# Casting loads of v on GpSimd's queue, wider early ReLUs and paired score phases in a linear-attention and MLP kernel

## The chip, the cores and the metric

The kernel runs on one core of one Trainium2 chip. The metric is the device time in microseconds (us) of one execution, smaller is better; where several executions were timed, the median is given. Two of the core's data paths matter here beside its compute engines: SP (SyncE) issues DMAs on one queue (q1 in the profile), GpSimd (POOL) issues them on another (q0).

## The reference

Two stages are computed, one after the other. Shapes: 4 batches, 8 heads, 768 steps, head size 48; 3072 tokens of 384 features, hidden size 2048. All inputs and the output are float32.

```python
def _attn_ref(q, k, v, alpha):
    state = np.zeros((B, H, D, D), dtype=np.float32)
    for t in range(S):
        state = alpha[:, :, t, :, None] * state + np.einsum('bhd,bhe->bhde', k[:, :, t], v[:, :, t])
        y[:, :, t] = np.einsum('bhd,bhde->bhe', q[:, :, t], state)
    return y

def _moe_ref(x, w_in, w_out):          # x: y with the heads side by side
    r = np.maximum(x @ w_in, 0.0)
    return (r * r) @ w_out
```

## The kernel before

**Tiles.** The 3072 tokens are 24 chunks of 128 steps, six to a batch. For each chunk the recurrence is done in closed form: the logarithm of alpha is summed along the steps on TensorE, its exponential A scales q and the inverse Ainv scales k, masked products of the two give the weights of v within the chunk, and a state carried from chunk to chunk gives the rest. The result is transposed into `xT_big` and is the input of the MLP ("MoE" in the code).

**One chunk** (`add_chunk`) is a chain over the engines. The names are those of the planned operations: `e_ln` (ScalarE, L445); `p0`, the sums (TensorE); `e_A`, `e_Ai`, `e_ae0`, `e_ae1`, exponentials (ScalarE, L461 to L471); `e_qA`, `e_kI`, the scaled q and k (VectorE, L474 and L477; for the first four chunks `e_kI` may go to GpSimd); `p1`, their transposes (TensorE), copied by `e_cp`; `p2`, the scores, eight matmuls of 64 rows (TensorE, L521); `e_sm`, the causal mask on the scores, two multiplies of 512 columns (VectorE, L536); `ps`, the state's update, then `e_stm` and `e_sb`; `p3`, mask times v plus q times state; `e_xn`; `p4`, the transposes; `e_xT`. v is read by `ps` and `p3` in bfloat16: `e_vb` (L441) casts the loaded float32 tile on GpSimd.

**The first four chunks** share a start of their own (`four_slots`): alpha and q of the first 512 steps come as two larger loads each (`slot_at`, `slot_qt`, L322), four steps to a partition, so that the sums of all four chunks are made at once. The order of these chunks' operations is written out by hand as priorities in the table `RANK`.

**The MLP.** Tokens are taken in groups of one or two chunks (`GN`). In `add_moe1` one *fill* is three matmuls of up to 256 columns into a PSUM bank for one of 16 blocks of the hidden size, followed by a ReLU on ScalarE (`e_relu`, L640) and a square on VectorE (`e_sq`, L646) into `gT`. In `add_moe2` sixteen matmuls of 384 columns per token tile make the output, which is copied out of PSUM (`e_ev`, L678) and stored by SP (L683). All matmuls are recorded at the helper's line L225, transposes at L228.

**Loads and queues.** `add_loads` issues at, qt, kt and vt (alpha, q, k, v) of a chunk, 192 KB each, from SP (L336); chunks 4 and 5 are issued by GpSimd through `pool_dma`, which keeps GpSimd's loads in a chain. The weights are loaded by GpSimd as well, cast to bfloat16 on the way, in four quarters each (`load_w`, L289). `hold_w` (L304) holds the first weight load until chunk 2's keys have landed; `hold_x` (L310) holds chunk 6's alpha, the first of SP's later loads, until chunk 5's keys have landed. Each of the four load tiles has `LB = 5` buffers.

**What sets the order.** Every operation is an `Op` with an engine, an assumed duration, what it depends on and a priority. `Plan.run` walks through time with these durations and takes on each engine whatever can start first, then by priority; the resulting order is emitted and pinned, so each engine runs its instructions in that fixed order and waits where the chip differs from the plan. Seven PSUM banks are handed out by the same plan: from chunk 6 on, the linear attention uses banks 0 and 1 (`GLA_BANKS`) for `p0`, `p1`, `p3` and `p4`, and banks 5 and 6 (`sl_sc`) for the scores; the MLP uses the three between. A chunk may start only `LEAD = 4` chunks ahead of the MLP's progress (`gate`).

Of the kernel before, what the change touches and what calls it, by code (L numbers as in the profile page):

```python
# [8 lines left out]
FP32 = mybir.dt.float32  # L9
# [101 lines left out]
def kernel(  # L111
# [32 lines left out]
    LB = 5  # L144
    loads = ctx.enter_context(tc.tile_pool(name="loads", bufs=LB))
# [81 lines left out]
    def tr(*a):  # L227
# [4 lines left out]
        "ps0": -59.649, "kI0": -59.644, "xn2": -57.597, "stm2": -57.593, "vb1": -57.593, "vb3": -57.587,  # L232
        "cpq2": -57.587, "Ai1": -57.583, "pq1": -57.579, "stm0": -55.864, "kI2": -52.641, "qA2": -52.000,
        "sm0": -51.992, "cp2": -51.977, "xT3": -51.974, "sm3": -51.974, "A0": -49.635, "qA0": -49.458,
        "xn1": -49.452, "pk": -48.562, "p42": -48.558, "p13": -48.116, "p43": -47.738, "xT2": -47.629,
        "qA1": -45.851, "cp1": -45.808, "cpq3": -44.752, "ae0": -42.850, "ae1": -42.842, "cpq0": -42.695,
        "sb1": -40.290, "vb0": -39.263, "p21": -37.946, "pq2": -37.716, "kI3": -37.711, "p33": -37.384,
        "xT1": -37.379, "ps1": -37.280, "tq2": -36.745, "pq3": -36.029, "cp0": -33.098, "sb2": -33.092,
        "ln1": -32.725, "kI1": -32.161, "A3": -32.154, "tq1": -32.145, "stm1": -31.966, "Ai3": -31.587,
        "p40": -31.579, "p30": -31.562, "p32": -30.816, "A1": -29.621, "tq0": -23.589, "qA3": -23.487,  # L240
        "sb0": -23.373, "Ai2": -23.199, "pq0": -22.649, "ln0": -22.507, "sm2": -22.167, "sb3": -20.897,
        "p41": -20.599, "sm1": -18.297, "A2": -15.473, "p12": -13.495, "vb2": -13.438, "Ai0": -12.640,
        "p23": -12.616, "ps3": -12.587, "xn0": -11.830, "cp3": -10.020, "p20": -10.018, "pae": -10.015,
        "xT0": -9.291, "tq3": -8.768, "p22": -7.414, "stm3": -7.367, "p11": -7.059, "ps2": -5.829, "p31":
        -5.636, "p10": -4.409, "cpq1": -2.002, "xn3": -0.260,
# [32 lines left out]
    hold = consts.tile([P, 1], FP32)  # L278
    w_gate = []

    def pool_dma(dur, issue, emit, *deps):

        i = add("POOL", issue, emit, *deps, *w_gate, prio=-50.0, lat=0.0)
        w_gate[:] = [i]
        return add("DMA", dur, lambda: None, i, lat=2.0)
# [16 lines left out]
    def hold_w(d, nm):  # L302
        def e_hold():
            pin(nc.gpsimd.tensor_copy(hold, d[nm][:, 0, 0:1]))  # L304
        w_gate[:] = [add("POOL", 0.1, e_hold, d["ld_" + nm], prio=-6.0)]

# [5 lines left out]

    C = [dict() for _ in range(NT)]
# [3 lines left out]
    def load_tile(nm):  # L317
        return loads.tile([P, H, D], FP32, name=nm)

    def load_slots(nm, lo, hi):  # L320
        def ld():
            pin(nc.sync.dma_start(out=slot[nm][:, lo:hi].rearrange("p h j d -> p h (j d)"),  # L322
                                  in_=slot_srcs[nm][:, lo:hi]))
        return add("DMA", 2.4 * (hi - lo) / H, ld, lat=2.0, at=0.9)

    def add_loads(s, names=("at", "qt", "kt", "vt"), pool=False):
        d = C[s]
        b, c = divmod(s, NCH)
        for nm, src in srcs:
            if nm not in names:  # L330
                continue

            def ld(nm=nm, src=src):
                if nm not in d:
                    d[nm] = load_tile(nm)
                pin((nc.gpsimd if pool else nc.sync).dma_start(out=d[nm], in_=src[b, c]))  # L336
            m = made[nm]
            prev = C[m[-LB]]["use_" + nm] if len(m) >= LB else None
            m.append(s)
            if pool:  # L340
                d["ld_" + nm] = pool_dma(LD, X_ISSUE, ld, prev)
# [3 lines left out]
    def four_slots(ld_at, ld_qt):  # L345
# [19 lines left out]
        pks = add("PE", 1.0, e_pk, *pk, key="pk", prio=-31.0)  # L365
# [26 lines left out]
        for j in range(NJ):  # L392
# [23 lines left out]
            pq = e["pq_"] = add("PE", 0.65, e_pq, *lns, takes=sl_all, key=f"pq{j}", **h)  # L416
# [8 lines left out]
    def add_chunk(s):  # L425
# [13 lines left out]
        def e_vb():  # L439
            d["vb"] = work.tile([P, H, D], BF16, name="vb", bufs=4)  # L440
            pin(nc.gpsimd.tensor_copy(d["vb"], d["vt"]))  # L441
        vb = d["use_vt"] = add("POOL", 0.52, e_vb, d["ld_vt"], old, key=key("vb"), prio=-60.0 if s < 6 else -5.0)
# [46 lines left out]
        if first:  # L489
            lo = NP  # L490
            ae1 = d["aes"]
            mk = d["use_kt"] = add({"DVE": 0.47, "POOL": 0.92}, 0, e_kI, d["ai"], d["ld_kt"], key=key("kI"), **g)
# [44 lines left out]
        if s < 6:  # L537
            p2s = [add("PE", 0.3, lambda hh=hh: e_p2h(hh), cp, *q_ready, takes=sl_all, key=key("p2"), **g) for hh in range(2)]
            sm_after = p2s
        else:  # L540
            p2s = [plan.add(Op("PE", 0.0, lambda hh=hh: e_sc_bank(hh), [cp], takes=[sl_sc[hh]], lat=0.0, **g)) for hh in range(2)]
            sm_after = [add("PE", 0.42, e_p2, *p2s, **g)] * 2
# [5 lines left out]
        if not last:  # L548
            def e_ps():
# [3 lines left out]
                for p in range(NP):  # L553
                    mm(st[:, p, :], lhsT=kI[:, 2 * p:2 * p + 2, :], rhs=d["vb"][:, 2 * p:2 * p + 2, :],
# [16 lines left out]
        def e_p3():  # L571
# [5 lines left out]
            for hh in range(2):  # L577
                for p in range(NP):
                    h = 2 * p + hh
                    mm(py[:, h * D:(h + 1) * D], lhsT=d["sm"][:, hh, p, :], rhs=d["vb"][:, h, :],  # L580
# [22 lines left out]
        d["end"] = d["x"]  # L603

# [20 lines left out]
    def add_moe1(g, f, before):  # L625
        t0, n = GT[g] * P, GN[g] * P
        box = {}

        def e_mm():
            prog_t = box["ph"] = psum(op, [P, 512], FP32)  # L630
# [163 lines left out]
```

## Time and profile before

| | |
|---|---|
| median of 9 runs | 194.36 us (191.01 to 195.92) |
| the profiled execution | 193.66 us, of which the profile's span is 192.0 us |
| TensorE matmul (PE) busy | 180.8 us, 94% of the span |
| VectorE (DVE), ScalarE (ACT), GpSimd (POOL) busy | 140.2, 132.9, 33.9 us |
| first MoE matmul | at 20.88 us of the span |
| last matmul's output copy | starts at 188.46 us |
| loads of at, qt, kt, vt by SP | 18, 18, 22, 22 |
| casts of v on GpSimd | 24, 14.3 us in all |
| ReLUs | 208, 70.3 us in all |

The profile shows one execution. "Busy" sums the instructions of an engine without double counting; the end of a matmul is modelled, so starts are the firmer numbers. Times inside the span start at its zero; 1.66 us of the execution lie outside it. The chain is read backwards from the last instruction: at each step it names what released it.

### The profile page before, as it was taken

What the parts mean: (1) busy time and instruction counts of PE and PEld (TensorE: products, weight loads), DVE (VectorE), ACT (ScalarE), POOL (GpSimd) and SP (SyncE); (2) the same over time, 40 slices, a digit from 0 to 9 for tenths busy, and PEclk for the clock granted to TensorE, in tenths of its full rate; (3) what the DMA queues carried; (4) which work ended last, traced back from release to release, by engine and by line L of the source; (5) the groups of instructions that cost most, each with busy time, mean ns of one, the idle gap of its engine ahead of it and who ended that gap; (6) DMA issues with size and microseconds to landing.
All of it is one profiled execution on the core that took longest, in us unless ns stands there. A gap on an engine that the chain in (4) does not pass through costs nothing.

```text
span 192.0 us, 5309 instructions
## 1 busy us (share of the span) xinstructions
PE 180.8 (94%) x1973; PEld 133.8 (70%) x1973; DVE 140.2 (73%) x380; ACT 132.9 (69%) x393; POOL 33.9 (18%) x64
## 2 busy tenths in 40 slices
PE   7769899999989996999999999999999999999992
PEld 2346688667776874777777787787777777777751
DVE  3199778548999996787888888888798887754400
ACT  3665799356895985787787788688787677556610
POOL 7079835211011211111111011011010000000000
PEclk9999999999999999999999999999999999999999
DMA  6997999959978997999999847845011011011112
GB/s 183 241 199 116 174 205 236 239 116 224 234 169 169 203 229 144 209 203 231 208 202 224 175 104 162 160 104 151 5 41 41 3 41 42 3 41 46 41 41 82
DMA packets 93017, 27.07 MB, mean 141 GB/s; under 512 B 83904, under 2 KB 92608, under 8 KB 92992
## 3 DMA queue, kind: packets, MB, share of 16 engines
q1 hardware_dynamic: 88768, 22.03, 51.6%
q0 software_dynamic: 4224, 4.72, 14.2%
q8 instruction: 15, 0.25, 0.6%
q14 instruction: 10, 0.08, 0.1%
HBM read 25.17 MB, written 4.72 MB: 156 GB/s over the span
## 4 chain that ended last, share of the span: by engine, by line
PE 82%; DMA 8%; SPq 4%; ACT 2%; POOL 1%; issue 1%; ACTq 0%
PE bank L225 75%; PE bank L228 6%; DMA w_in_b<-in_moe_w_in_dram 3%; DMA at<-in_alpha_dram 3%; SPq L336 3%; DMA vt<-in_v_dram 2%; PE st L225 1%; SPq L322 1%; ACT r L640 1%; POOL kI_s L477 1%; POOL vb L441 1%; ACT L_s L445 0%; ACT xn L219 0%; ACT ob L678 0%; ACT A L461 0%
## 5 line engine op out<-in xcount | busy, mean ns | idle before, releaser
L640 ACT ACTIVATE r<-bank 128x256 bf16<-128x256 f32 (+1 forms) x208 | 70.3, 373 | 27.4 <-PE bank L225 26.7
L225 PE MATMUL bank<-xT_big,w_in_b 128*128 128x256 bf16 (+1 forms) x624 | 79.8, 264 | 1.7 <-DMA w_in_b<-in_moe_w_in_dram 0.8
L225 PE MATMUL bank<-w_out_b,gT 128*128 128x384 bf16 x384 | 75.0, 326 | 0.0
L646 DVE TENSOR_TENSOR gT<-r 128x256 bf16<-128x256 bf16 (+1 forms) x208 | 55.5, 289 | 14.8 <-ACT r L640 13.2
L225 PEld LDWEIGHTS <-w_in_b 128*128 128x128 bf16 x624 | 52.8, 97 | 10.1 <-issue 1.0
L225 PEld LDWEIGHTS <-gT 128*128 128x128 bf16 x384 | 36.8, 98 | 16.5
L441 POOL CAST vb<-vt 128x384 bf16<-128x384 f32 x24 | 14.3, 597 | 94.6 <-PE bank L225 59.4
L536 DVE TENSOR_TENSOR sm<-bank,utri_b 128x512 bf16<-128x512 f32 x40 | 27.0, 685 | 3.8 <-PE bank L225 3.8
L217 DVE COPY qkT<-bank 128x1024 bf16<-128x1024 bf16 (+1 forms) x21 | 14.2, 675 | 6.0 <-PE bank L228 6.0
L678 ACT COPY ob<-bank 128x384 f32<-128x384 f32 x21 | 10.0, 478 | 10.5 <-PE bank L225 10.5
L474 DVE TENSOR_TENSOR qA_s<-qt,A 128x384 bf16<-128x384 f32 x20 | 11.4, 572 | 6.4 <-ACT A L461 6.3
L225 PEld LDWEIGHTS <-qkT 64*128 64x128 bf16 (+1 forms) x260 | 10.4, 95 | 7.0 <-DVE gT L646 3.8
L568 ACT CAST sb<-st 128x384 bf16<-128x384 f32 x20 | 9.6, 481 | 5.4 <-DVE st L563 5.3
L445 ACT ACTIVATE L_s<-at 128x384 bf16<-128x384 f32 x20 | 10.3, 522 | 3.4 <-DMA at<-in_alpha_dram 3.1
L477 DVE TENSOR_TENSOR kI_s<-kt,Ainv 128x384 bf16<-128x384 f32 x22 | 12.1, 549 | 0.4 <-ACT Ainv L465 0.3
L219 ACT CAST xn<-bank 128x384 bf16<-128x384 f32 x22 | 10.8, 491 | 1.6 <-PE bank L225 1.5
L563 DVE TENSOR_TENSOR st<-st,ae_s 128x384 f32<-128x384 f32 x20 | 11.1, 556 | 0.7 <-PE st L225 0.7
L461 ACT ACTIVATE A<-bank 128x384 bf16<-128x384 f32 x20 | 9.9, 497 | 1.0 <-PE bank L225 1.0
L465 ACT ACTIVATE Ainv<-bank 128x384 bf16<-128x384 f32 x20 | 10.5, 525 | 0.0
L228 PE MATMUL bank<-ident_bf,qA_s 128*128 128x128 bf16 x96 | 9.3, 219 | 1.2 <-DVE qA_s L407 0.8
L228 PEld LDWEIGHTS <-qA_s 128*128 128x128 bf16 x96 | 6.9, 98 | 4.0 <-DVE qA_s L407 2.0
L225 PE MATMUL bank<-vb,sm 128*128 128x48 bf16 x192 | 9.0, 184 | 0.4 <-DVE sm L536 0.3
(77 smaller groups left out, 158.7 us busy)
## 6 DMA issues: line engine op xcount, KB each, us to landing
out_dram<-ob SPq DMA_DIRECT2D x24, 192.0 KB, 2.9
kt<-in_k_dram SPq DMA_DIRECT2D x22, 192.0 KB, 3.7
vt<-in_v_dram SPq DMA_DIRECT2D x22, 192.0 KB, 3.9
at<-in_alpha_dram SPq DMA_DIRECT2D x18, 192.0 KB, 4.1
qt<-in_q_dram SPq DMA_DIRECT2D x18, 192.0 KB, 3.7
w_in_b<-in_moe_w_in_dram POOLq DMA_DIRECT2D x4, 384.0 KB, 7.6
w_out_b<-in_moe_w_out_dram POOLq DMA_DIRECT2D x4, 384.0 KB, 11.1
slot_at<-in_alpha_dram SPq DMA_DIRECT2D x2, 384.0 KB, 3.8
```

The source lines that it names most:

```text
L217: pin(nc.vector.tensor_copy(out, in_))
L219: pin(nc.scalar.copy(out, in_))
L225: pin(nc.tensor.matmul(*a, **kw))
L228: pin(nc.tensor.transpose(*a))
L441: pin(nc.gpsimd.tensor_copy(d["vb"], d["vt"]))
L465: pin(nc.scalar.activation(d["Ai"], d["pm"][:, 0:HD].rearrange("p (h d) -> p h d", h=H), AF.Exp, scale=-1.0))
L474: pin(nc.vector.tensor_mul(qA[:, :, 0:D], d["qt"], d["A"]))
L477: pin((nc.vector if mk.eng == "DVE" else nc.gpsimd).tensor_mul(kI[:, :, 0:D], d["kt"], d["Ai"]))
L536: pin(nc.vector.tensor_mul(d["sm"][:, hh], d["sc"][hh], (utri_p if first else utri_b).to_broadcast([P, NP, P])))
L563: pin(nc.vector.tensor_mul(st4, st4, bcast(ae, D)))
L640: pin(nc.scalar.activation(box["r"][:, 0:n], box["ph"][:, 0:n], AF.Relu))
L646: pin(nc.vector.tensor_mul(gT[g][:, f, 0:n], box["r"][:, 0:n], box["r"][:, 0:n]))
```

## The change

- **v.** `e_vb` and the float32 tile of v are gone. v is loaded into a bfloat16 tile (`LBV = 6` buffers) and cast by the DMA, for all 24 chunks from GpSimd's queue. From chunk 6 on, a one-column copy on GpSimd stands ahead of each such load and makes it wait for the previous chunk's keys; the buffer is free when `p3` of six chunks before is done.
- **The start.** Chunk 3's keys are issued by GpSimd too, ahead of v3 and of the weights; `hold_w` is gone, the four quarters of `w_in` follow at once. `e_kI` of the first four chunks stays on VectorE. `RANK` is replaced. Ten more dummy matmuls, of 128 columns, follow the nine of 512 at the start.
- **Chunk 6** is held until chunk 5's alpha has landed, not its keys.
- **ReLUs.** In the first five groups (`g < M1_ALT`) `nf` fills go side by side into one bank of 512 columns (two fills for groups of two chunks, four for groups of one), then one ReLU and one square take them all.
- **Scores.** From chunk 10 on (`PAIRS`), the scores of an even chunk and of the next are made in one phase, sixteen matmuls one after the other; the even chunk's use banks 5 and 6, the odd one's banks 0 and 1.
- **The last output tile** is made in two halves of 192 columns, each over all sixteen blocks. The second half is copied out by VectorE and ScalarE, 96 columns each, and stored from two queues.
- Some assumed durations of the plan change slightly.

```diff
+    LBV = 6
...
     RANK = {
...
-    def hold_w(d, nm):
-        def e_hold():
-            pin(nc.gpsimd.tensor_copy(hold, d[nm][:, 0, 0:1]))
-        w_gate[:] = [add("POOL", 0.1, e_hold, d["ld_" + nm], prio=-6.0)]
...
+    PAIRS = 10
     def load_tile(nm):
+        if nm == "vt":
+            return loads.tile([P, H, D], BF16, name=nm, bufs=LBV)
         return loads.tile([P, H, D], FP32, name=nm)
...
             def ld(nm=nm, src=src):
                 if nm not in d:
                     d[nm] = load_tile(nm)
-                pin((nc.gpsimd if pool else nc.sync).dma_start(out=d[nm], in_=src[b, c]))
+                if nm == "vt" and after:
+                    pin(nc.gpsimd.tensor_copy(d[nm][:, 0, 0:1], after["kt"][:, 0, 0:1]))
+                pin((nc.gpsimd if pool or nm == "vt" else nc.sync).dma_start(out=d[nm], in_=src[b, c]))
...
-        def e_vb():
-            d["vb"] = work.tile([P, H, D], BF16, name="vb", bufs=4)
-            pin(nc.gpsimd.tensor_copy(d["vb"], d["vt"]))
-        vb = d["use_vt"] = add("POOL", 0.52, e_vb, d["ld_vt"], old, key=key("vb"), prio=-60.0 if s < 6 else -5.0)
+        vb = d["ld_vt"]
...
-            mk = d["use_kt"] = add({"DVE": 0.47, "POOL": 0.92}, 0, e_kI, d["ai"], d["ld_kt"], key=key("kI"), **g)
+            mk = d["use_kt"] = add("DVE", 0.47, e_kI, d["ai"], d["ld_kt"], key=key("kI"), **g)
...
+            second = s % 2
+            p2s = [add("PE", 0.0, lambda hh=hh: e_sc_bank(hh), cp, takes=[(GLA_BANKS if second else sl_sc)[hh]],
+                       lat=0.0, **g) for hh in range(2)]
+            if second:
+                p2 = C[s - 1]["p2"]
+                for o in C[s - 1]["p2s"]:
+                    o.deps.append(cp)
+                p2.deps += p2s
+                p2.both = e_p2
+            else:
+                def e_both():
+                    e_p2()
+                    p2.both()
+                p2 = add("PE", 0.63, e_both, *p2s, **g)
...
+    def moe1_fill(g):
+        return 512 // (GN[g] * P) if g < M1_ALT else 1
...
         def e_relu():
-            box["r"] = rpool.tile([P, 512], BF16, name="r")
-            pin(nc.scalar.activation(box["r"][:, 0:n], box["ph"][:, 0:n], AF.Relu))
+            box["r"] = rpool.tile([P, nf, n], BF16, name="r")
+            pin(nc.scalar.activation(box["r"], box["ph"], AF.Relu))
...
+    def add_last_tile(g, tt, before):
+        w = d_model // 2
+        for half in range(2):
...
+            parts = [("DVE", 0, w)] if half == 0 else [("DVE", 0, w // 2), ("ACT", w // 2, w // 2)]
...
     for s in range(NJ):
-        add_loads(s, ("kt", "vt"))
-        if s == 3:
-            hold_w(C[2], "kt")
-            load_w_in(0)
+        add_loads(s, ("kt", "vt"), pool=s == NJ - 1)
...
-    for x in "iiioo4oo5":
+    for x in "iiiioo4oo5":
...
-    hold_x(C[6], C[5], "kt")
+    hold_x(C[6], C[5], "at")
     for s in range(6, NT):
-        add_loads(s)
+        add_loads(s, after=C[s - 1])
...
     dummies(9, 0.0, 1.0)
+    dummies(10, 0.0, 1.0, 128)
```

## The prediction

> **What bounds the kernel now.** I read the page first (busy shares, chain), then the chain in order of time, the idle time of TensorE by stage, the DMA by stage, and single starts in a steady stretch.
>
> ```profile
> PE 180.8 (94%) x1973; PEld 133.8 (70%) x1973; DVE 140.2 (73%) x380; ACT 132.9 (69%) x393; POOL 33.9 (18%) x64
> ...
> PE 82%; DMA 8%; SPq 4%; ACT 2%; POOL 1%; issue 1%; ACTq 0%
> ```
>
> TensorE is busy 94% of the span and holds 82% of the chain that ended last. Only three things are worth anything: an earlier start of its dense stretch, fewer gaps in it, less work in it; and then the tail. The chain in order of time:
>
> ```profile
> 14.24 0.39 POOL vb L441
> 14.63 6.21 DMA w_in_b<-in_moe_w_in_dram
> 20.84 0.05 issue
> 20.88 1.15 PE bank L225 x6
> ...
> 68.14 5.77 DMA at<-in_alpha_dram
> 73.91 0.02 issue
> ...
> 74.48 0.49 ACT xn L219
> 74.97 0.05 issue
> 75.02 0.34 PE bank L228 x3
> ```
>
> The first MoE matmul (20.88) waits for the first quarter of w_in, which GpSimd issued only at 14.63, behind four v and k steps. From there to 188.44 the chain is TensorE almost without a break. The one long break is at 75.02: an alpha tile was issued at 68.14 and landed at 73.91; the Ln waited for it and the xn cast stood behind the Ln on ScalarE. By stage (columns: PE, PEld, DVE, ACT, POOL, granted clock, DMA share, GB/s):
>
> ```profile
> 10.00:12.00 2.00, 1.27 (x24) 0.87 (x21) 2.00 (x3) 1.50 (x4) 1.67 (x2) 1.00 1.00 196
> ...
> 14.00:16.00 2.00, 1.69 (x32) 1.31 (x32) 1.91 (x4) 0.97 (x2) 2.00 (x5) 1.00 0.61 122
> ...
> 36.00:38.00 2.00, 2.00 (x22) 1.44 (x21) 0.60 (x1) 0.00 (x0) 0.00 (x0) 1.00 1.20 284
> ...
> 40.00:42.00 2.00, 2.00 (x27) 1.39 (x26) 0.49 (x1) 0.73 (x2) 0.70 (x2) 1.00 0.09 16
> ...
> 47.00:57.00 10.00, 9.32 (x154) 7.68 (x152) 9.68 (x35) 8.95 (x38) 0.60 (x1) 1.00 0.90 204
> 57.00:67.00 10.00, 9.75 (x121) 7.57 (x118) 9.68 (x32) 7.68 (x27) 1.51 (x3) 1.00 0.97 188
> 67.00:76.00 9.00, 7.46 (x97) 5.39 (x95) 7.00 (x19) 5.88 (x19) 0.54 (x2) 1.00 0.89 182
> ...
> 93.48:100.55 7.07, 7.07 (x84) 5.40 (x82) 5.92 (x15) 5.50 (x17) 0.87 (x2) 1.00 1.01 209
> ```
>
> TensorE is idle 0.68, 0.25 and 1.54 us in the three stages from 47 to 76, with 0.09 before: 2.56 in all. From 76 on it is full, 7.07 us for a chunk. The clock is 1.00 throughout. The DMA engines have two holes, at 15.1 to 16.5 (loads done, weights not begun) and at 39.6 to 41.9 (chunk 6 held back until chunk 5's keys had landed).
>
> **The change, part by part.**
>
> *Start.* SP issues 7 loads instead of 12; GpSimd, free from 4.47, issues v0, v1, v2, k3, v3 at 0.90 each (its rows for at, qt, kt, vt) and reaches w_in at 4.5 + 5 x 0.90 = 9.0 instead of 14.63, with no cast or hold before it. Before, by the DMA packets of the trace, the weights' data flowed from 16.5 and the first quarter ended at 19.25, landing 1.6 later. Closing the hole gives 1.4. Loads of 192-byte rows moved at 196 GB/s on SP's queue (10 to 12 us) and at 284 on GpSimd's (36 to 38): 0.196 MB is 1.00 us there and 0.69 here, and five loads moved save another 1.5. The quarter could land at 20.84 - 2.9 = 17.9. But the matmul also needs the transposed outputs of chunks 0 and 1, and their copies end at 20.0. So the weights alone give 0.9, and more only if VectorE, full from 10 to 20, gets there sooner:
>
> ```profile
> 10.22 1.87 DVE L407 TENSOR_TENSOR qA_s<-slot_qt,A 128x384 bf16<-128x384 f32 x2
> 10.46 1.22 POOL L477 TENSOR_TENSOR kI_s<-kt,Ainv 128x384 bf16<-128x384 f32 x1
> ```
>
> Beside a GpSimd product, two qA take 1.87 us where two others take 2 x 0.56. With the third (0.85 at 12.48) that is 1.04 us lost to overlap. All kI now go to VectorE: two more at 0.55 are 1.10, so its total stays; but kI0 no longer takes 1.22 us on GpSimd behind a 0.50 us cast. I take 1.2 for the start. Ends: -0.8 if the new hand order of the first four chunks is worse by one VectorE score product (0.68) and a little; +2.4 if chunks and weights both come early. The ten extra short dummy matmuls cost nothing: a 512-column one takes 0.425 there, so ten of 128 end at about 6.2, before the logarithms at 6.29; without that cover, at most 1.1.
>
> *v on GpSimd's queue later.* 24 casts (14.3 us) leave GpSimd and 22 issues of 0.89 (two were there) enter it, each behind a column copy (0.19) that waits for the previous chunk's keys. Queued behind that wait is only the next v. v is read late in a chunk: of the one whose Ln starts at 73.93 the transposes that come before any use of v start at 78.87. Cost on TensorE nothing; the cover is these 5 us in the tight stage (more in the steady one, where loads run ahead), and beyond it every us late is a us of TensorE. For the other tensors it is a gain: chunk 6's alpha now waits for chunk 5's alpha only. The load stream comes forward by the two holes, 1.4 + 2.3 = 3.7, and by 0.3 a chunk as v moves faster. The Ln at 73.93 was late by 2.76; this covers it, so the 1.54 goes. I take 1.5; ends 0 (another wait takes its place) and 1.54.
>
> The Trainium skill's page "SBUF — State Buffer", section "SBUF: two separate sides" with its box on the trap "DVE blocks DMA", speaks against this: while VectorE runs an operation that uses both ports, GpSimd can't write descriptors, and a load it measured at 620 ns became 3100. As an estimate by that page, five loads each 2.5 us late ahead of the weights would add 12 us to the start. This trace doesn't agree: GpSimd's issues take 0.92, 0.92, 0.92 and 0.89 at 19.8 to 23.9 with VectorE over two thirds busy; so the sum goes by these rows.
>
> *ReLUs.* For the first five groups one ReLU covers 512 columns: 80 become 32. In line, 14 of 256 take 4.62, 0.33 each, and 5 of 128 take 1.14, 0.23 each. Logarithms of 768 and 384 columns take 0.84 and 0.52, so 0.83 ns a column, and one of 512 is 0.33 + 0.21 = 0.54. ScalarE saves 24 x (0.66 - 0.54) + 8 x (0.92 - 0.54) = 5.9 us between 21 and 70; the squares shrink likewise. That is worth at most the gaps left there, 2.56 - 1.54 = 1.0, put down to ScalarE's ReLU (0.54 and 0.25 are the largest). I take 0.6; ends 0 and 1.0. Against it stands that a bank comes free only after its second fill.
>
> *Scores by two.* A score phase costs fixed time:
>
> ```profile
> 101.21 0.81 PE L225 MATMUL bank<-w_out_b,gT 128*128 128x384 bf16 x4
> ...
> 101.96 0.40 PE L225 MATMUL bank<-qkT 64*128 64x128 bf16 x8
> ...
> 102.29 0.83 PE L225 MATMUL bank<-xT_big,w_in_b 128*128 128x256 bf16 x6
> ```
>
> The four matmuls end at 101.21 + 4 x 0.163 = 101.86 (40 of them take 6.6 at the end), so the phase takes 0.43 until 102.29. Its eight start by pairs 0.056 apart: 0.22 of work, 0.21 of change-over. Chunks 10 to 23 make 7 pairs and drop 7 change-overs: 7 x 0.20 = 1.4, all on the bound engine. Ends: 1.5 and below nothing (first rival).
>
> *Tail.* The last tile is done in two halves, and what follows the last matmul shrinks from a 384-column copy to 96 columns on each of two engines and two small stores:
>
> ```profile
> 188.46 0.48 ACT L678 COPY ob<-bank 128x384 f32<-128x384 f32 x1 [2.12 <-PE bank L225]
> ```
>
> 288 columns fewer at 0.83 ns are 0.24; the store, 2.9 to landing at 192 KB, may lose up to 0.4. I take 0.4; ends 0 and 0.6. The halves need 32 matmuls of 192 columns instead of 16 of 384, the same columns; 128-column ones start 0.056 apart, so loading weights doesn't bind.
>
> *New waits.* The order of every engine is planned anew and v's and the pair's constraints are new: I charge 0.7, about a quarter of today's gaps; ends 0 and 2.
>
> **Sum.** 1.2 + 1.5 + 0.6 + 1.4 + 0.4 - 0.7 = 4.4 us. The profiled execution took 193.66 with a span of 192.0; 187.6 + 1.66 = 189.3. That execution lies 0.7 under the median of the nine runs, 194.36, so against the median I forecast 190.0. All best ends together give 7.0, 187.3; all worst ones -2.8, 197.2. The likeliest case's own range is 187.3 to 192.4, up to where it can still be told from no change. The nine runs reach from 191.0 to 195.9; about 1%, 1.9 us, is what a measurement of this kernel can tell from no change.
>
> **Rivals.**
>
> 1. *The pair chokes the two banks of the linear attention; slower.* The second chunk's scores lie in the same two banks that p0, p1, p3 and p4 use. They stay taken until VectorE has masked both chunks: 4 x 0.685 = 2.74 us. If the next such matmul stands on TensorE only one pair of MoE steps later (0.66 + 0.65 = 1.3), TensorE idles 1.4 for each pair: 7 x 1.4 = 10.1 lost against 3.0 of other gains, 201.4. It decides from 0.7 a pair on (4.9 - 3.0 = 1.9). For it: both banks at once. Against: 74% of TensorE's time is MoE work that needs neither bank. 0.12.
> 2. *The start gives nothing or costs.* VectorE is full there and the matmul waits for chunks, not weights: start -0.8, sum 2.4, 192.0. For it: only 0.9 lay between the copies and the weights. 0.15.
> 3. *The waits move.* Other gaps replace both those closed, and pairs give half: 1.2 + 0.4 + 0.7 - 0.7 = 1.6, 192.8. Against it: the DMA holes are plainly avoidable. 0.10.
> 4. *v comes late*, as issue waits on the keys before it and has only GpSimd's queue. Beyond the 5 us of cover each of the six tight chunks costs the excess; 1 us each makes 6 - 4.4 = +1.6, 196.0, and more makes it slower. Against: the issue rows. 0.05.
>
> **How the numbers follow.** The forecast has 0.58, all faster. Rival 2 lies at the bound, 0.08 faster and 0.07 same; rival 3 is 0.03 and 0.07; rivals 1 and 4 are slower, 0.17. So faster 0.69, same 0.14, slower 0.17. Range 187.0 to 195.5: some 0.05 lies below, 0.14 above.
>
> **What would show it.** Right: the first MoE matmul before 20; no DMA hole at 15 or 40; no Ln waiting over 1 us for alpha; a pair of chunks near 13.95 us instead of 14.14 in the steady stretch; under 3.3 us from the last matmul to the end. Wrong: TensorE idle after masks in the pair stages, or behind v; GpSimd's issues well over 0.9; a first MoE matmul after 21.

## The result, and the profile after

The kernel became a little faster, by less than was forecast: the median of 21 executions is 191.58 us (190.30 to 195.94), that of the kernel before, timed beside it, 194.06 (63 executions), which is 2.48 us or 1.3% less. The ratio is 0.9927, with a 95% interval of 0.9898 to 0.9955; it is formed from those executions alone that ran in the faster of two states of the chip, and so isn't the quotient of the two medians. A second series of the unchanged file gave 190.50 us (6 executions) and a ratio of 0.9886 (0.9839 to 0.9932). Forecast were 190.0 us, 2.2% less; by the first ratio a third of that came, by the medians somewhat over half.

The profiled execution took 190.1 us with a span of 188.4. The page, lines of the busy shares, the granted TensorE clock by fortieths of the span, the two DMA queues and the chain by engine:

```profile
PE 180.3 (96%) x1999; PEld 137.2 (73%) x1999; DVE 132.3 (70%) x335; ACT 126.6 (67%) x346; POOL 41.9 (22%) x78
...
PEclk9996599999999999999999999999999999999999
...
q1 hardware_dynamic: 64992, 17.45, 43.9%
q0 software_dynamic: 29120, 6.88, 38.0%
...
PE 87%; DMA 5%; SPq 2%; DVE 1%; ACT 1%; issue 1%; ACTq 0%; DVEq 0%
```

TensorE's share of the chain rose from 82% to 87%. The clock is at half between 16 and 23 us, which it was not before. The DMA share of the chain was weights, alpha and v before (3.2, 3.0 and 2.0%) and is k alone now. The chain in order of time, its beginning and the step into the dense stretch:

```profile
3.48 2.15 SPq L339
5.68 9.41 DMA kt<-in_k_dram
15.59 0.56 DVE st L578
16.15 1.10 DVE sm L533 x2
17.30 0.58 DVE st L578
...
22.31 14.48 PE bank L226 x139
```

The first MoE matmul comes at 22.31 instead of 20.88, and what it goes back to is chunk 2's keys: issued by SP at 5.68, landed 9.41 us later, at 15.09. VectorE in order of time shows who waited (in brackets the idle time and what ended it):

```profile
12.01 0.56 DVE L474 TENSOR_TENSOR kI_s<-kt,Ainv 128x384 bf16<-128x384 f32 x1 [0.41 <-DMA kt<-in_k_dram]
12.49 0.75 DVE L218 COPY qT<-bank 128x512 bf16<-128x512 bf16 x2
15.12 0.56 DVE L474 TENSOR_TENSOR kI_s<-kt,Ainv 128x384 bf16<-128x384 f32 x1 [1.88 <-DMA kt<-in_k_dram]
15.59 0.56 DVE L578 TENSOR_TENSOR st<-st,ae_s 128x384 f32<-128x384 f32 x1
16.06 1.28 DVE L533 TENSOR_TENSOR sm<-bank,utri_p 128x512 bf16<-128x512 f32 x2
```

The order on VectorE is fixed: k2's product (at 15.12) stands ahead of chunk 0's state and mask, and the two, which need nothing of k2, wait behind it. In the kernel before, k2's product was done by GpSimd, and VectorE did chunk 0's state at 14.17 and the first masks right behind it:

```profile
12.96 1.14 POOL L477 TENSOR_TENSOR kI_s<-kt,Ainv 128x384 bf16<-128x384 f32 x1
...
14.17 0.56 DVE L563 TENSOR_TENSOR st<-st,ae_s 128x384 f32<-128x384 f32 x1
14.81 2.48 DVE L536 TENSOR_TENSOR sm<-bank,utri_p 128x512 bf16<-128x512 f32 x4
```

From there on the changed kernel gains. The stages of the tight stretch and a pair of chunks in the steady one (columns as before: length, PE, PEld, DVE, ACT, POOL, clock, DMA share, GB/s):

```profile
40.00:42.00 2.00, 2.00 (x24) 1.35 (x23) 0.42 (x1) 0.90 (x2) 0.00 (x0) 1.00 1.71 193
...
47.00:57.00 10.00, 9.83 (x169) 8.30 (x167) 9.38 (x21) 7.75 (x20) 1.60 (x5) 1.00 1.32 213
57.00:67.00 10.00, 10.00 (x135) 7.93 (x133) 8.65 (x21) 7.79 (x21) 2.98 (x5) 1.00 1.33 188
67.00:76.00 9.00, 9.00 (x94) 6.92 (x92) 7.07 (x17) 7.24 (x20) 2.12 (x4) 1.00 1.39 182
...
97.32:111.26 13.94, 13.94 (x164) 10.89 (x161) 11.23 (x31) 10.61 (x33) 2.13 (x5) 1.00 0.82 130
```

TensorE's idle time in the three stages fell from 2.47 us (29 less 9.32, 9.75 and 7.46) to 0.17. The DMA hole at 40 is gone (share 0.09 before, 1.71 now). A pair of chunks takes 13.94 us instead of 2 x 7.07.

Two measures serve for the rest of this document. **By equal progress** means: the difference between two kernels of the moment at which the same number of MoE columns has been streamed by TensorE. **Stalls** are the times from one matmul's start to the next one's, less what its columns need (0.422 ns each, as 384-column ones start 0.162 us apart), summed where more than 0.05 us is left. By equal progress the changed kernel is 1.43 us late at its first MoE columns, 1.81 late at about 30 us, 3.03 early at the end: 1.81 lost at the start, 4.84 won later. The stalls from 30 us on went from 7.85 to 3.05 us.

### The profile page after: what moved, and what is told of

It is laid out like the page before. It is cut to its first block, busy times and chain, and to the rows that moved or that the text cites. A ratio compares the mean times of both kernels' runs of the same rounds, so it can differ in the third digit from the quotient of the medians.

```text
span 188.4 us, 5215 instructions
## 1 busy us (share of the span) xinstructions
PE 180.3 (96%) x1999; PEld 137.2 (73%) x1999; DVE 132.3 (70%) x335; ACT 126.6 (67%) x346; POOL 41.9 (22%) x78
## 4 chain that ended last, share of the span: by engine, by line
PE 87%; DMA 5%; SPq 2%; DVE 1%; ACT 1%; issue 1%; ACTq 0%; DVEq 0%
PE bank L226 78%; PE bank L229 7%; DMA kt<-in_k_dram 5%; PE st L226 2%; SPq L339 1%; SPq L319 1%; ACT r L668 1%; DVE st L578 1%; DVE sm L533 1%; ACT sb L583 0%; ACT xn L220 0%; DVE ob L736 0%; ACT ob L736 0%; ACT L_s L442 0%; DVE kI_s L474 0%
## 5 line engine op out<-in xcount | busy, mean ns | idle before, releaser
L668 ACT ACTIVATE r<-bank 128x256 bf16<-128x256 f32 (+1 forms) x160 | 64.7, 429 | 29.3 <-PE bank L226 27.8
L226 PE MATMUL bank<-w_out_b,gT 128*128 128x384 bf16 (+1 forms) x400 | 74.7, 320 | 0.0
L675 DVE TENSOR_TENSOR gT<-r 128x256 bf16<-128x256 bf16 (+1 forms) x160 | 47.5, 314 | 15.4 <-ACT r L668 13.8
L226 PEld LDWEIGHTS <-gT 128*128 128x128 bf16 x400 | 37.9, 98 | 15.8
L533 DVE TENSOR_TENSOR sm<-bank,utri_b 128x512 bf16<-128x512 f32 x40 | 25.3, 683 | 2.6 <-PE bank L226 2.5
L339 POOL DMA_DIRECT2D vt<-in_v_dram x24 | 21.3, 888 | 8.2 <-POOL vt L338 6.1
L338 POOL CAST vt<-kt 128x1 bf16<-128x1 f32 x18 | 4.2, 233 | 64.7 <-PE bank L226 40.5
L218 DVE COPY qkT<-bank 128x1024 bf16<-128x1024 bf16 x20 | 13.7, 687 | 4.9 <-PE bank L229 4.9
L474 DVE TENSOR_TENSOR kI_s<-kt,Ainv 128x384 bf16<-128x384 f32 x24 | 13.3, 555 | 3.3 <-DMA kt<-in_k_dram 2.8
L229 PE MATMUL bank<-ident_bf,kI_s 128*128 128x128 bf16 x96 | 9.5, 223 | 2.2 <-DVE kI_s L474 2.2
L218 DVE COPY xT_big<-bank 128x384 bf16<-128x384 bf16 x20 | 7.0, 352 | 4.2 <-PE bank L229 3.7
## 6 DMA issues: line engine op xcount, KB each, us to landing
out_dram<-ob SPq DMA_DIRECT2D x23, 192.0 KB, 3.0
kt<-in_k_dram SPq DMA_DIRECT2D x21, 192.0 KB, 5.0
at<-in_alpha_dram SPq DMA_DIRECT2D x18, 192.0 KB, 5.1
qt<-in_q_dram SPq DMA_DIRECT2D x18, 192.0 KB, 4.3
```

The costliest lines, as they stand in the source:

```text
L218: pin(nc.vector.tensor_copy(out, in_))
L226: pin(nc.tensor.matmul(*a, **kw))
L229: pin(nc.tensor.transpose(*a))
L339: pin((nc.gpsimd if pool or nm == "vt" else nc.sync).dma_start(out=d[nm], in_=src[b, c]))
L474: pin((nc.vector if mk.eng == "DVE" else nc.gpsimd).tensor_mul(kI[:, :, 0:D], d["kt"], d["Ai"]))
L533: pin(nc.vector.tensor_mul(d["sm"][:, hh], d["sc"][hh], (utri_p if first else utri_b).to_broadcast([P, NP, P])))
```

## The experiments

All times are medians; a single execution is one look and only its trace is read. Expectations are quoted as they were written before each run.

### The same file again

No edit.

> The changed kernel once more, to stand beside the others on one chip. Its first profile: first MoE matmul at 22.31 us, k2 landing at 15.1, clock 0.982 (half speed for 6.83 us from about 16.1), 190.1 us. All theories: about the same, 190 to 192 by chance of the start, 0.5 to 1.5% under the kernel before.

Measured: 190.50 us, ratio 0.9886 (0.9839 to 0.9932); span 188.7, first MoE matmul at 22.47. The loss at the start is in this profile too.

### The old start in the changed kernel

```diff
-        "sm0": -56.473, "cpq1": -50.279, ...
+        "ps0": -59.649, "kI0": -59.644, ...
...
+            hold_w(C[2], "kt")
+            load_w_in(0)
...
+        if first:
+            vb = add("POOL", 0.52, e_vb, d["ld_vt"], key=key("vb"), prio=-60.0)
...
-            mk = d["use_kt"] = add("DVE", 0.47, e_kI, d["ai"], d["ld_kt"], key=key("kI"), **g)
+            mk = d["use_kt"] = add({"DVE": 0.47, "POOL": 0.92}, 0, e_kI, d["ai"], d["ld_kt"], key=key("kI"), **g)
```

> The start of before put back into the changed kernel: first four v loaded by SP and cast on GpSimd, k3 by SP, weights held behind k2, old hand order, kI on either engine. All else as changed. Theory A (the new start costs what it was to save): first MoE matmul back to 20.9, clock 1.00, 1.4 to 1.8 us faster than the changed kernel: 188.3 to 188.7 in a profile. Rival (the start is worth little either way, the loss lies later): within 0.5 us of the changed kernel.

Measured: 192.84 us, ratio 0.9949 (0.9910 to 0.9989), span 189.7. A miss. The start itself came near what was expected: the first MoE matmul is at 21.37 (20.9 expected), and by equal progress it is 1.35 us ahead of the changed kernel at about 30 us; the clock, expected full, was at half for 3.41 us from 12.95. But it ends 1.17 us behind: 2.52 are lost again later. Its stalls from 30 us on are 5.63 us against 3.05, all of them of less than 0.3. The whole order comes out of one plan, and with another start it is another order later too: at 70 us of the changed kernel, by equal progress, 12 fewer matmuls of the linear attention have been done. So undoing the start doesn't price the start alone, and every comparison below is made by equal progress, at the start and at the end apart.

### Is it the half clock?

TensorE's idle 1.6 us at 14 to 16 is followed by a half clock. Dummy matmuls of 512 columns were put into the gap, two ahead of chunk 1's transposes and seven ahead of chunk 2's:

```diff
+            n = {"p11": 2, "p12": 7}.get(op.key if hasattr(op, "key") else None, 0)
+            dummies(n, op.start, op.start)
```

> The changed kernel with nine dummy matmuls of 512 columns more, two ahead of the transposes of k1 and seven ahead of those of k2, where TensorE waits for the keys. Loads as changed. Theory A (idle TensorE, then half clock): k2 still lands near 15, the clock stays 1.00, the 6.8 us at half speed go, first MoE matmul at 20.5 to 21.3, 1 to 1.8 us faster than the changed kernel. Rival B (VectorE and the new order set the start, the clock is only beside it): the clock may rise, but the first MoE matmul stays after 21.8 and the time within 0.5 us.

Measured: 191.46 us, ratio 0.9882 (0.9820 to 0.9943), span 188.4. The stages of this kernel, with the granted clock in the last column but two:

```profile
14.00:16.00 2.00, 2.00 (x23) 0.88 (x17) 0.45 (x1) 0.11 (x1) 1.32 (x2) 1.00 1.36 194
16.00:18.00 2.00, 1.16 (x17) 0.76 (x16) 2.00 (x5) 0.97 (x2) 1.21 (x2) 1.00 1.25 210
18.00:20.00 2.00, 1.57 (x23) 1.03 (x20) 2.00 (x5) 0.86 (x2) 0.94 (x2) 1.00 1.24 203
```

The clock is full, and the first MoE matmul is still at 22.49; by equal progress it is 0.03 us ahead of the changed kernel from 30 us to the end. So the half clock isn't the main loss: VectorE is full (2.00 of 2.00) as soon as k2 has landed, and idle ahead of it:

```profile
15.55 0.56 DVE L474 TENSOR_TENSOR kI_s<-kt,Ainv 128x384 bf16<-128x384 f32 x1 [1.89 <-DMA kt<-in_k_dram]
```

It may still cost a part. In this execution k2's product starts 0.43 us later than in the changed kernel's (15.12), and no progress is lost by it. Counted from that product, this kernel is 0.46 us ahead at 30 us; against the second profile of the changed kernel (product at 15.29) it is 0.63. An estimate from these three executions is that the half clock accounts for about half a microsecond of the 1.81.

### Is it the landing, or the order behind it?

Four kernels. The first holds what GpSimd issues after v2 until k2 has landed:

```diff
+    def hold_w(d, nm):
...
+        if s == NJ - 1:
+            hold_w(C[2], "kt")
         add_loads(s, ("kt", "vt"), pool=s == NJ - 1)
```

> The changed kernel with GpSimd's k3, v3 and the weights held until k2 has landed (a one-column copy on GpSimd). Theory A (GpSimd's loads take the DMA engines from SP's keys): k2 lands by 13 instead of 15.1, no idle stretch of TensorE over 1 us, clock 1.00, first quarter of w_in landing at 19 to 20.5, first MoE matmul at 20 to 20.8: 1.5 to 2.3 us faster than the changed kernel. Rival B (VectorE and the new order): k2 earlier, but the first MoE matmul stays after 21.8.

Measured: 192.80 us, ratio 0.9980 (0.9948 to 1.0012), span 191.0. k2 landed at 14.27, only 0.8 earlier, with v0 to v2 still beside it; VectorE's work on chunks 0 and 1 came 0.8 to 0.9 earlier; the weights were issued only at 16.58 and landed at 21.83, and the first MoE matmul stayed at 22.23. Later another 2.8 us are lost, most of it as stalls at 70 to 80 us (2.22 against 0.19). So holding the queue was no cure.

The second moves no load. The plan is told that k1 and k2 come later, as the trace shows, and so places other work ahead of their products:

```diff
-                d["ld_" + nm] = add("DMA", LD, ld, ..., lat=2.0, at=0.9)
+                late = {("kt", 1): 1.2, ("kt", 2): 2.3}.get((nm, s), 0.0)
+                d["ld_" + nm] = add("DMA", LD, ld, ..., lat=2.0 + late, at=0.9)
```

> The changed kernel, but its plan is told that k1 lands 1.2 us and k2 2.3 us later than it assumed, so VectorE's fixed order puts the masks and the state of chunk 0 ahead of the product of k2. No load is moved. Theory E (k2 lands at 15.1, and VectorE, whose next instruction is that product, stands 1.9 us before it with everything behind): no VectorE wait over 0.7 us between 13 and 17, first MoE matmul at 20.2 to 21.0 instead of 22.3, 1.2 to 2.0 us faster than the changed kernel (188.4 to 189.2 in a profile). Rival F (what counts is when the data of chunks 2 and 3 lands, or the half clock): first MoE matmul stays after 21.8, time within 0.5 us.

Measured: 187.56 us, ratio 0.9694 (0.9636 to 0.9752), span 185.1: the fastest kernel of this study, and faster than both. VectorE in order of time:

```profile
12.05 0.55 DVE L475 TENSOR_TENSOR kI_s<-kt,Ainv 128x384 bf16<-128x384 f32 x1
12.69 1.29 DVE L534 TENSOR_TENSOR sm<-bank,utri_p 128x512 bf16<-128x512 f32 x2
13.89 0.56 DVE L579 TENSOR_TENSOR st<-st,ae_s 128x384 f32<-128x384 f32 x1
14.36 0.55 DVE L475 TENSOR_TENSOR kI_s<-kt,Ainv 128x384 bf16<-128x384 f32 x1
14.82 1.28 DVE L534 TENSOR_TENSOR sm<-bank,utri_p 128x512 bf16<-128x512 f32 x2
...
16.48 0.55 DVE L475 TENSOR_TENSOR kI_s<-kt,Ainv 128x384 bf16<-128x384 f32 x1
```

Chunk 0's masks start at 12.69 instead of 16.06. The product at 14.36 is k3's, whose keys had landed at 14.24; k2's, at 16.48, is now the last, and those of k1, k2 and k3 wait for nothing. k2 itself landed at 14.97, only 0.12 us earlier than in the changed kernel. The first MoE matmul comes at 19.05, 3.26 us earlier than in the changed kernel, and by equal progress the two stay 3.3 us apart to the end: the later order is the same. This is more than the 1.2 to 2.0 expected: 0.38 of it was there at chunk 0's keys (product at 9.25 instead of 9.63), and the clock stayed full, as TensorE no longer idles. The rest is VectorE's order behind k2, which was the loss: k2 came as late as ever. With the order put right, the start is 1.5 us ahead of the kernel before at 30 us, near the 1.2 that was forecast for it.

The third moves k2 to GpSimd's queue, ahead of v2:

```diff
-        add_loads(s, ("kt", "vt"), pool=s == NJ - 1)
+        add_loads(s, ("kt", "vt"), pool=s >= NJ - 2)
```

> The changed kernel with k2 issued by GpSimd too, ahead of v2, so that SP has only k0 and k1. Theory E: k2 lands by 13.5, VectorE waits under 0.7 us for it, first MoE matmul at 20.3 to 21.3, 1 to 2 us faster than the changed kernel. Rival G (the DMA engines are full from 2 to 15 us whatever the queue, and what is moved ahead pushes another load back): k2 after 14.3 or another tensor as late, first MoE matmul after 21.8, time within 0.5 us.

Measured: 189.36 us, ratio 0.9825 (0.9750 to 0.9899), first MoE matmul at 21.57, 0.96 us ahead by equal progress. Now k1's product waits 1.41 us, until 13.26, and k2's stands at 14.40 with no wait. The wait moved from one key tile to the other and became shorter.

The fourth tells the plan larger delays (the edit is shown against the second):

```diff
-                late = {("kt", 1): 1.2, ("kt", 2): 2.3}.get((nm, s), 0.0)
+                late = {("kt", 1): 2.2, ("kt", 2): 5.0}.get((nm, s), 0.0)
```

> The changed kernel with the plan told that k1 comes 2.2 us and k2 5.0 us later than it assumes (no load is moved): the landings that the slower of the executions showed. Theory E (the order on VectorE, not the landing itself, sets the start): k2's product goes behind all of chunk 0's and chunk 1's work, so nothing waits for k2 and the time is that of the plan told 1.2 and 2.3 us, 187.0 to 188.0 us, with fewer executions above 190. Rival P (a plan made for late keys delays chunk 2's own work, and this comes back as a wait after the first MoE matmuls): 188.5 to 190 us, with stalls of TensorE between 20 and 60 us.

Measured: 188.41 us, ratio 0.9760 (0.9694 to 0.9826), span 186.7. k2's product, now at 17.84, waits for nothing, but the kernel is no faster: in its profile it is 1.07 us behind the plan with 1.2 and 2.3 us at 30 us and 1.60 at the end. Of the 1.07, 0.66 was there at chunk 0's keys already (its product starts at 9.91 instead of 9.25, after a wait for them), which no order of k1 and k2 can mend. The time lies between the ranges of E and P, and P's stalls between 20 and 60 us are not there (2.2 us against 2.4 with the smaller delays); 0.65 us more of stalls after 30 us (3.70 against 3.05) come later, and what causes them stays open. Even so this start, with chunk 0's keys later than in the changed kernel, is 2.24 us ahead of it at 30 us. Five of the six executions lie between 188.22 and 188.81.

### Why k2 lands at 15 us

First guess: the casting v loads. In the trace a casting load of v moves as 1024 packets of 96 bytes (4096 for the four of the start), at a median of 29 ns each. So the first four v were loaded as float32 instead, and cast by GpSimd afterwards:

```diff
+        if nm == "vt" and s < NJ:
+            return loads.tile([P, H, D], FP32, name="vf", bufs=NJ)
...
+            vb = add("POOL", 0.52, e_vb, d["ld_vt"], key=key("vb"), prio=-60.0)
```

> The changed kernel with the first four v loaded by GpSimd's queue as float32, without a cast on the way, and cast on GpSimd afterwards; hand order, queues and weights as changed. In the profiles so far a 96-byte casting packet of v took 30 ns of a DMA engine against 16 for a 192-byte packet on SP's queue: 1.9 us a load over 16 engines instead of 1.0. Theory H (the casting loads of v fill the DMA engines and hold k1 and k2 back): v's packets come larger and the DMA share between 7 and 14 us falls, k2 lands by 13.7 instead of 15.1, first MoE matmul at 20.5 to 21.7, 0.8 to 1.8 us faster than the changed kernel (188.7 to 189.7). Rival I (any second queue beside SP's does this, cast or not): k2 still after 14.7, time within 0.5 us.

Measured: 200.99 us, ratio 1.0324 (1.0248 to 1.0399), span 197.7: slower than the kernel before, and the largest miss of the study; the first MoE matmul came at 31.16. The keys became later still:

```profile
17.59 0.56 DVE L481 TENSOR_TENSOR kI_s<-kt,Ainv 128x384 bf16<-128x384 f32 x1 [4.81 <-DMA kt<-in_k_dram]
...
23.94 0.56 DVE L481 TENSOR_TENSOR kI_s<-kt,Ainv 128x384 bf16<-128x384 f32 x1 [5.13 <-DMA kt<-in_k_dram]
```

Its float32 v go from GpSimd's queue as packets of 3840 and 4224 bytes, at 336 and 367 ns (medians). So it isn't casting that makes k late, but what shares the engines with it; beside the larger packets fewer of SP's packets of 192 bytes get through. The next kernel leaves SP's queue alone, by holding everything of GpSimd's behind k2:

```diff
+    def hold_w(d, nm):
...
     for s in range(NJ):
-        add_loads(s, ("kt", "vt"), pool=s == NJ - 1)
+        if s < NJ - 1:
+            add_loads(s, ("kt",))
+    hold_w(C[2], "kt")
+    for s in range(NJ):
+        add_loads(s, ("vt",) if s < NJ - 1 else ("kt", "vt"), pool=s == NJ - 1)
```

> Changed kernel, but nothing at all starts on GpSimd's queue (v0 to v2, k3, v3, the weights) before k2 has landed: SP's loads have the DMA engines to themselves. Theory N (SP's packets of 192 bytes crawl because GpSimd's queue has its own packets on the same engines; three doses so far: casting packets of 30 ns beside them, k2 at 15.1 us; float32 packets of some 270 ns, 23.9 us; in the kernel before, nothing beside them, 12.96 us at the latest): from 6 us on some 3600 packets of SP's queue are left, and alone that queue moved 3057 to 3171 packets in 3 us in the kernel before, so k2 lands at 10 to 11 us, 12 at the latest. Rival O (k2 is late by its own issue, or by a spread between executions that has nothing to do with the other queue): 14 to 15 us as in the changed kernel. Both: v and the weights start some 7 us later than in the changed kernel, so the first MoE matmul comes at 23 to 26 us and the time is 192 to 197 us; the landing of k2 alone decides.

Measured: one look, 192.39 us, span 190.7, first MoE matmul at 22.71. GpSimd's hold, which reads k2, shows the landing:

```profile
11.21 0.56 POOL L305 COPY hold<-kt 128x1 f32<-128x1 f32 x1 [6.74 <-DMA kt<-in_k_dram]
```

k2 is there at 11.2, in the place that theory N gave it (10 to 11, 12 at the latest), 3.9 us earlier than in the changed kernel, though SP issued it at the same time (5.76, against 5.68). The same is seen in the queues' packets. DMA by queue (packets, MB, time as a share of 16 engines) in the stretch from 9 to 12 us, in the kernel before, in the first of the four kernels above (`hold_w` ahead of k3, so that only v0 to v2 run beside k), and in the changed kernel:

```profile
q1 hardware_dynamic: 3057, 0.58, 97.9%
```

```profile
q0 software_dynamic: 2075, 0.20, 123.4%
q1 hardware_dynamic: 1264, 0.24, 55.3%
```

```profile
q0 software_dynamic: 2176, 0.37, 156.2%
q1 hardware_dynamic: 617, 0.12, 33.7%
```

and from 12 to 15 us in the kernel with float32 v:

```profile
q0 software_dynamic: 264, 0.50, 93.8%
q1 hardware_dynamic: 226, 0.04, 14.8%
```

Alone, SP's queue moves some 1000 packets of 192 bytes a microsecond; beside GpSimd's 96-byte packets alone 421, beside these and 41 packets of 3840 and 4224 bytes, which are k3's, 206, and beside 86 such large ones and 142 of the weights' 1024 bytes 75. So k3's move to GpSimd's queue has a part in it too, though holding k3, v3 and the weights back brought k2 forward by 0.8 us only. In the kernel before, the first packet of GpSimd's queue starts at 16.3 us, after the last of SP's first loads (15.4): with v on SP's queue and the weights behind `hold_w`, the two never met there, and it was this that the change gave up. Packet size and bytes moved change together in these kernels, and how the engines choose between the queues was not tried.

The landing also varies between executions: in the kernel without pairs below, whose start is the changed kernel's, k2's product waited until 19.21. What sets this spread stays open, and so does its share in the medians: only single executions were traced.

Two dummies ahead of the transposes of chunks 1, 2 and 3 in the fastest kernel, against its own executions at 190 and 191 us:

```diff
+            n = {"p11": 2, "p12": 2, "p13": 2}.get(op.key if hasattr(op, "key") else None, 0)
+            dummies(n, op.start, op.start)
```

> late_plan with two dummy matmuls of 512 columns ahead of the transposes of each of k1, k2 and k3. late_plan ran at 186.8 to 187.6 with the clock at 1.00 and at 190.4 and 191.4 with 0.97. Theory J (in those two TensorE idled for a load and the half clock then cost the 3 us): clock at 0.99 or more in nearly all runs and all of them under 188.5. Rival K (the loads come late in such runs and the clock only shows it): the spread stays, some runs over 190 with the clock near 1.00.

Measured: 189.06 us (187.85 to 193.93), ratio 0.9721 (0.9654 to 0.9789). No gain; the profile is 1.06 us behind the fastest kernel's from the start to the end. Dummies at 17.89 stand ahead of the state's matmuls, and VectorE waits for these until 19.00. The two longest executions, 191.49 and 193.93, still have a lower granted clock (0.981 and 0.964, against 0.998 to 1.000 in the other four), so neither J (nearly all at full clock and under 188.5 us) nor K (some over 190 at full clock) came true.

### What each later part is worth

In these kernels, as in the changed one, the clock is at half for some time before 29 us and full from there to the last matmul, so the parts from 30 us on can be compared.

No scores by two:

```diff
-    PAIRS = 10
+    PAIRS = NT
```

> The changed kernel with the scores of each chunk in a phase of their own again. The prediction's term: 7 change-overs of 0.20 us, so a pair of chunks takes 14.14 us instead of 13.94 and the span is 1.4 us longer, with the start as in the changed kernel. Rival (the saving is lost elsewhere, as two banks stay taken): span within 0.5 us of the changed kernel's 188.4 to 188.7.

Measured: one look, 196.81 us, span 195.1, with k2 late as told above. By equal progress the distance to the changed kernel is 4.98 us from 30 to 72 us, before any pair (the changed kernel's first comes at 78.6), and 6.71 at the end: the seven pairs are worth 1.73 us, 0.25 each.

One ReLU per fill:

```diff
     def moe1_fill(g):
-        return 512 // (GN[g] * P) if g < M1_ALT else 1
+        return 1
```

> The changed kernel with one ReLU and one square for each fill again. The prediction's term: the gaps of TensorE put down to ReLUs between 45 and 60 us come back, span 0.6 to 1.0 us longer. Rival (these gaps went for another reason, the earlier loads): within 0.3 us.

Measured: one look, 194.42 us, span 192.7. By equal progress 1.06 us are lost at the start (the landing again) and 4.31 at the end, so 3.25 by the ReLUs. The stage:

```profile
57.00:67.00 10.00, 8.73 (x129) 7.12 (x127) 9.90 (x39) 8.97 (x36) 3.87 (x6) 1.00 1.45 184
```

TensorE is at 8.73 instead of 10.00, VectorE at 9.90, and fills wait on TensorE for the ReLU that frees their bank:

```profile
57.54 0.50 PE L226 MATMUL bank<-xT_big,w_in_b 128*128 128x128 bf16 x6 [0.23 <-ACT r L668]
58.26 0.33 PE L226 MATMUL bank<-xT_big,w_in_b 128*128 128x128 bf16 x3 [0.23 <-ACT r L668]
```

The hold on chunk 6, tried from both sides, in the kernel before and in the changed one:

```diff
-    hold_x(C[6], C[5], "kt")
+    hold_x(C[6], C[5], "at")
```

> The kernel before with chunk 6's alpha held until chunk 5's alpha has landed, not its keys: the earlier load stream alone. The prediction's term: the DMA hole at 40 us closes, the Ln near 74 us no longer waits 2.8 us, TensorE's gap of 1.5 us there goes, span 1.2 to 1.6 us shorter than 192.0. Rival L (with one ReLU a fill, ScalarE is the next limit between 45 and 70 us and the gap comes back as waits for ReLUs): shorter by 0.5 us or less.

```diff
-    hold_x(C[6], C[5], "at")
+    hold_x(C[6], C[5], "kt")
```

> The changed kernel with chunk 6's alpha held until chunk 5's keys have landed, as before. The prediction's term: the load stream starts 2 us later and up to 1.5 us of TensorE's time comes back as a wait for alpha. Rival M (with v off SP's queue the stream has room enough): from the first MoE matmul to the end within 0.3 us of the changed kernel's.

Measured: one look each. In the kernel before (196.74 us, span 194.9) the start was 3.36 us late and the end 2.94: the earlier alpha gives 0.42. The stalls at 70 to 80 us shrink from 1.89 to 0.65, but those at 50 to 70 grow from 2.50 to 3.46 and those at 90 to 100 from 0.19 to 0.85. In the changed kernel (191.35 us, span 189.6) the start was 0.65 late and the end 1.24: the old hold costs 0.59.

## Why the prediction was right and wrong

**The direction was right, the size was not.** By its own sum, against the profiled execution, it forecast 4.4 us; the profiles show 3.52 by progress and tail. Between the medians 2.48 are left (194.06 less 191.58); why less than between the profiles isn't shown. That the median still lies inside the stated range, 187.0 to 195.5, is partly luck: the start came out 3.0 us worse than its term, and the stages behind it 2.0 better than theirs.

| term | forecast | measured |
|---|---|---|
| start | +1.2 | -1.81 (first MoE matmul -1.43) |
| loads, ReLUs, pairs, less new waits | 1.5 + 0.6 + 1.4 - 0.7 = 2.8 | 4.84 |
| of these: hold on chunk 6, undone alone | (of 1.5) | 0.42 and 0.59 |
| ReLUs, undone alone | 0.6 (0 to 1.0) | 3.25 |
| pairs, undone alone | 1.4 (below 0 to 1.5) | 1.73 |
| tail | 0.4 (0 to 0.6) | 0.49 (3.54 to 3.05 us) |
| sum | 4.4 | 3.52 |

**The start was the failed step**, and outside its own ends (-0.8 to +2.4). The sign that the prediction named for this, a first MoE matmul after 21, came (22.31). The weights did come early, as forecast: GpSimd issued the first quarter at 8.85 (forecast 9.0) and it landed at 17.12 (forecast 17.9), although the hole in the DMA work that was reckoned at 1.4 us is 0.9 by the packets (15.4 to 16.3). But the matmul waited for chunks 0 and 1, as rival 2 said ("VectorE is full there and the matmul waits for chunks, not weights"). Rival 2's time, 192.0, is near the median, but by luck: it was sized by one mask product in the wrong place and didn't see a wait for a load. Two links were missing. The prediction reckoned that the moved loads "save another 1.5" in moving v at 0.69 us a load; shown is that SP's k pays for GpSimd's traffic (k2 at 11.2 alone, at 15.1 with it, at 23.9 beside larger packets). And it counted k's products on VectorE as busy time only ("its total stays"), not as places in a fixed order, where a product behind a late load holds back all that follows. That second link is the decisive one: with no load moved and k2 landing within 0.12 us of its old time, the order brings back 3.3 us, of which 0.38 was there at chunk 0's keys by chance and about half a microsecond can be put down to the clock.

The v loads themselves are not faster by casting. The 0.69 us assumed came from rows at 36 to 38 us, whose packets were up to 4224 bytes; a casting load goes as 1024 packets of 96 bytes, and the first two, alone on the engines in the kernel that held them back (13.4 to 15.8 us), took 1.2 us each, against 1.00 on SP's queue. The time of the two queues' packets was 65.8% of the 16 engines' 192.0 us before and 81.9% of 188.4 after. No gap of over 0.3 us on TensorE, VectorE or ScalarE after 22 us is ended by v: rival 4 (v late) did not happen.

**The ReLU term was mis-sized by its bound.** The 1.0 was what the idle column of the kernel before left in three stages. In the changed kernel, taking the wide ReLUs away brings 3.2 us of stalls back (6.26 against 3.05). The idle column sees only gaps that the modelled ends of matmuls leave open; the stalls from start to start, 7.85 us in the kernel before, were the truer stock. That the denser loads made ScalarE and VectorE tighter too, and so the ReLUs worth more, is argued, not shown.

**Right by their own steps** were the pairs (7 x 0.20 forecast, 7 x 0.25 measured; 13.94 us for a pair of chunks, forecast 13.95; rival 1's choke is nowhere) and the tail. No Ln waits over 1 us for alpha, and the DMA hole at 40 is gone. The loads' 1.5 is only partly right: the hold alone gives 0.4 to 0.6, since other gaps take over, as rival 3 had it. What v's later loads on GpSimd's queue gave was not undone by itself. The terms undone alone add to more than 4.84 (1.73 + 3.25 + 0.59 = 5.57), so they overlap.

**The page on VectorE and GpSimd** ("SBUF — State Buffer" of the Trainium skill, section "SBUF: two separate sides") was set aside in the sum, and the issue rows bear that out. The page has VectorE's two-port operations hold up GpSimd's writing of descriptors. GpSimd's group of v issues, with its busy time and the mean of one in ns, shows 888 (the longest 1014), against the 890 forecast from the rows of before; which of these VectorE operations use both ports no run here shows, so the page itself is not tested:

```profile
L339 POOL DMA_DIRECT2D vt<-in_v_dram x24 | 21.3, 888 | 8.2 <-POOL vt L338 6.1 <-DMA w_in_b<-in_moe_w_in_dram 1.8 <-issue 0.2
```

## What to carry to other kernels

A load moved to another queue is not free for the loads that stay: count packets on both queues in the same stretch, and ask which small-packet load lands later and who reads it. In an order fixed by a plan, every instruction behind a DMA is a wait in the making; compare the assumed landing with the trace and put the product that needs it where it can be late. Undoing one part of a planned kernel re-plans the rest, so compare by equal progress, before and after the part, rather than by the end alone.

## What the hardware showed that was not expected

- One queue takes engine time from another. In 3 us SP's queue got 3057 packets of 192 bytes through alone, 1264 beside 96-byte packets of GpSimd's queue, 617 beside these and some of about 4 KB, and 226 beside more of the large ones. The time of one such packet changed less: a median of 15 ns alone, 24 in the changed kernel, and 15 again in the kernel with float32 v.
- A casting load of v was cut into 1024 packets of 96 bytes at a median of 29 ns; the same v without a cast went as 48 packets, of 3840 and 4224 bytes. The packets of a queue overlap (in the kernel that held v back they fill 182.9% of 16 engines' time from 15 to 18 us), so packets times duration overstates what a load costs.
- 1.6 us of idle TensorE in the start was followed by 6.8 us at half the granted clock. Without the idle time the clock stayed at 1.00, and the kernel was no faster, with its keys 0.4 us later. Which idle time is enough isn't settled: with the old start in the changed kernel the longest gap ahead of the half clock, after the first two us, was 0.79 us, and 3.41 us at half followed; the kernel before has a gap of the same length at 11.4 us and kept 1.00.
